# Linear attention on one core: every queue in a listed order, min and relu over two heads at once, copies and products in halves

## The chip, the core and the metric

The kernel runs on one core of a Trainium2 chip. The metric is the device time in microseconds (us) of one execution. The engines are PE (TensorE), ACT (ScalarE), DVE (VectorE), POOL (GpSimd) and SP, whose queue issues the DMA transfers. The program gives each engine a queue; each takes its instructions in the order written there and waits on semaphores for the others.

An execution is called slow when it is over 1.5% above the fastest of the same kernel; the slow ones of the changed kernel and its variants show a mean TensorE clock of about 0.96. Fast runs are compared with fast runs. The profile is a look at one of the executions; its "span" is about 1.8 us shorter than that execution's time.

## The reference

```python
B, H, S, D = 1, 32, 2048, 128            # q, k, v: bf16, normal * 0.05
def reference(q, k, v):
    phi_q = jnp.where(q > 0, q + 1, jnp.exp(q)) + 1e-6
    phi_k = jnp.where(k > 0, k + 1, jnp.exp(k)) + 1e-6
    kv  = jnp.einsum("bhsd,bhse->bhde", phi_k, v)
    z   = jnp.einsum("bhsd->bhd", phi_k)
    num = jnp.einsum("bhqd,bhde->bhqe", phi_q, kv)
    den = jnp.einsum("bhqd,bhd->bhq", phi_q, z)[..., None] + 1e-6
    return num / den
```

There are 32 heads, each with three loads of 512 KB and one store of 512 KB.

## The kernel before

phi is taken apart: phi(x) = min(exp(x), 1) + 1e-6 + max(x, 0). Both parts go through TensorE separately and add up in PSUM. Every head h needs the following work. The line numbers are those that the profiles show; they shift with the edits.

| work | engine | line before | line after |
|---|---|---|---|
| exp k (ek) | ACT | L190 | L320 |
| min of exp k, plus eps (em); relu k (rk) | DVE | L220; L222 | L304; L312 |
| copy v beside a column of ones (v1) | POOL | L236 | L349 |
| kv product, 32 matmuls (kv) | PE | L251 | L336 |
| copy of kv out of PSUM (kvs) | ACT | L215 | L342 |
| 16 transposes of q (T) | PE | L243 | L327 |
| exp q (eq); relu q, first half or all (rqa) | ACT | L194; L202 | L366; L369 |
| relu q, second half (rqb); min of exp q (emq) | DVE | L207; L227 | L372; L375 |
| numerator and denominator, 38 matmuls | PE | L259, L263, L265 | L268, L272, L274 |
| reciprocal (rA, rC), product over 12 or 4 tiles (fA, fC) | DVE | L293, L299 | L291, L295 |

In three heads of four, relu q is split between ACT and DVE; in every fourth, ACT takes all of it. The queues are filled by a loop, so an engine's order is the order of the calls in it:

```python
for i in range(NH):
    eq(i)                                # ACT
    ... rqa(i)                           # ACT (head 0 has extra work here; cut)
    if i + 1 < NH: kvs(i + 1)            # ACT
    if i + 2 < NH: ek(i + 2)             # ACT, two heads ahead
    if i >= 1:     f(i - 1, "A")         # DVE: rA, fA
    rqb(i); emq(i)                       # DVE
    if i >= 1:     f(i - 1, "C")         # DVE: rC, fC
    if i + 2 < NH: emrk(i + 2)           # DVE: min, relu of head i + 2
    if i + 1 < NH: T(i + 1)              # PE
    nA(i); nC(i)                         # PE: numerators, tiles 0-11 and 12-15
    if i + 2 < NH: kv(i + 2)             # PE
```

Two buffers hold each of exp k, relu k, v1, exp q, relu q and kvs. Eight slots hold loaded heads, six hold outputs. kv shares a PSUM bank with the numerators of tiles 14 and 15, so PE, ACT and DVE take turns on it. The v copy of head h waits for the kv product of h - 2 and for the numerator of h - 3:

```python
def v1(h):
    dep = [f"ldv{h}"]
    if h >= 2: dep += [f"kv{h - 2}"]
    if h >= 3: dep += [f"nA{h - 3}"]
    add("POOL", f"v1{h}", lambda e: e.tensor_scalar(v1_sb[:, h % 2, :, 0:D], v_sb[...], 1.0, 0.0,
        op0=ALU.mult, op1=ALU.add), dep)     # cut
```

Of the kernel before, what the change touches and what calls it, by code (L numbers as in the profile page):

```python
# [6 lines left out]
P = 128  # L7
# [8 lines left out]
class Program:  # L16
# [3 lines left out]
    def __init__(self, sem):  # L20
        self.sem = sem
        self.ops = {e: [] for e in ENGINES}
        self.where = {}
        self.count = {}
        self.sems = {}

    def add(self, eng, key, fn, deps=(), dma=None, inc=True):

        name = dma if dma is not None else eng
        if dma is not None or inc:  # L30
            self.count[name] = self.count.get(name, 0) + (16 if dma is not None else 1)
        if key is not None:
            assert key not in self.where, key
            assert dma is not None or inc
            self.where[key] = (name, self.count[name], eng, len(self.ops[eng]))
        self.ops[eng].append((fn, tuple(deps), name, (16 if dma is not None else 1) if (dma is not None or inc) else 0))

    def resolve(self):
        after = {}
        known = {e: {} for e in ENGINES}  # L40
        nxt = {e: 0 for e in ENGINES}
        cnt = {}
        self.plan = {e: [] for e in ENGINES}
        left = sum(len(o) for o in self.ops.values())
        while left:
            moved = False
            for e in ENGINES:
                while nxt[e] < len(self.ops[e]):
                    fn, deps, name, by = self.ops[e][nxt[e]]
                    need = [self.where[d] for d in deps]  # L50
                    if any((s, v) not in after for s, v, _, _ in need):
                        break
                    waits = {}
                    for s, v, _, _ in sorted(need, key=lambda t: -t[3]):
                        if known[e].get(s, 0) < v:
                            waits[s] = max(waits.get(s, 0), v)
                            for s2, v2 in after[(s, v)].items():
                                known[e][s2] = max(known[e].get(s2, 0), v2)
                    self.plan[e].append((fn, list(waits.items()), name, by))
                    if by:  # L60
                        cnt[name] = cnt.get(name, 0) + by
                        k = dict(known[e])
                        k[name] = max(k.get(name, 0), cnt[name])
                        after[(name, cnt[name])] = k
                    nxt[e] += 1
                    left -= 1
                    moved = True
            assert moved, {e: (nxt[e], self.ops[e][nxt[e]][1]) for e in ENGINES if nxt[e] < len(self.ops[e])}

    def emit(self, eng, engine):  # L70
        for fn, waits, name, by in self.plan[eng]:
            for s, v in waits:
                engine.wait_ge(self.get(s), v)
            ins = fn(engine)
            if by:
                ins.then_inc(self.get(name), by)

    def get(self, name):
        if name not in self.sems:
            self.sems[name] = self.sem()  # L80
        return self.sems[name]
# [16 lines left out]
def bass_standalone__linear_attn_elu__prompt_kernel(nc: bass.Bass, q: bass.AP, k: bass.AP, v: bass.AP, out: bass.AP):  # L98
# [8 lines left out]
    NO = 6  # L107
    LAG = 2

# [3 lines left out]
    with ExitStack() as es:  # L113
# [12 lines left out]
        em_sb, rk_sb = sb([P, 2, N]), sb([P, 2, N])  # L126
# [5 lines left out]
        ident, ones, epsr, one1 = sb([P, P]), sb([P, P]), sb([P, 3]), sb([P, 1])  # L132
# [4 lines left out]
        CO = 4 * 512  # L137

        def slot(t):
            if t < 12:  # L140
                return 512 * (t // 3) + NC * (t % 3)
            return CO + 512 * ((t - 12) // 2) + NC * ((t - 12) % 2)

        pr = Program(sem)
        add = pr.add
# [15 lines left out]
        def load(name, dst, src, h, freed):  # L161
            dep = [f"{f}{h - NI}" for f in freed] if h >= NI else []
            add("SP", f"ld{name}{h}", lambda e: e.dma_start(
                dst[:, h % NI].rearrange("p (j d) -> p j d", d=D), rows(src, h)), dep, dma=f"{name}{h % NI}")

        def loads(h):
            load("k", k_sb, kf, h, ["ek", "rk"])
            load("q", q_sb, qf, h, ["T"])
            load("v", v_sb, vf, h, ["v1"])

        def store(h):
            s = h % NO
            if h < NH - 1:
                add("SP", f"st{h}", lambda e: e.dma_start(rows(of, h), o_sb[:, s]), [f"fA{h}", f"fC{h}"], dma=f"o{s}")
            else:
                add("SP", None, lambda e: e.dma_start(rows(of, h)[:, 0:12, :], o_sb[:, s, 0:12]), [f"fA{h}"], dma=f"o{s}")
                add("SP", f"st{h}", lambda e: e.dma_start(rows(of, h)[:, 12:NT, :], o_sb[:, s, 12:NT]), [f"fC{h}"],
                    dma=f"o{s}")
# [3 lines left out]
        for h in range(NH + LAG):  # L182
            if h + NI < NH:
                loads(h + NI)
            if h >= LAG:
                store(h - LAG)


        def ek(h):
            add("ACT", f"ek{h}", lambda e: e.activation(em_sb[:, h % 2], k_sb[:, h % NI], ACT.Exp),  # L190
                [f"ldk{h}"] + ([f"kv{h - 2}"] if h >= 2 else []))

        def eq(h):
            add("ACT", f"eq{h}", lambda e: e.activation(emq_sb[:, h % 2], xT[:, :], ACT.Exp),  # L194
                [f"T{h}"] + ([f"nC{h - 2}"] if h >= 2 else []))
# [4 lines left out]
        def rqa(h):  # L200
            n = N // 2 if split(h) else N
            add("ACT", f"rqa{h}", lambda e: e.activation(rq_sb[:, h % 2, 0:n], xT[:, 0:n], ACT.Relu),  # L202
                [f"T{h}"] + ([f"nC{h - 2}"] if h >= 2 else []))

        def rqb(h):
            if split(h):
                add("DVE", f"rqb{h}", lambda e: e.tensor_scalar(  # L207
                    rq_sb[:, h % 2, N // 2:], xT[:, N // 2:], 0.0, None, op0=ALU.max),
                    [f"eq{h}"] + ([f"nC{h - 2}"] if h >= 2 else []))

        def rqs(h):
            return [f"rqa{h}"] + ([f"rqb{h}"] if split(h) else [])

        def kvs(h):
            add("ACT", f"kvs{h}", lambda e: e.activation(kvs_sb[:, h % 2], kv_ps, ACT.Copy),  # L215
                [f"kv{h}"] + ([f"nC{h - 2}"] if h >= 2 else []))

        def emrk(h):
            s = h % 2
            add("DVE", f"em{h}", lambda e: e.tensor_scalar(  # L220
                em_sb[:, s], em_sb[:, s], 1.0, EPS, op0=ALU.min, op1=ALU.add), [f"ek{h}"])
            add("DVE", f"rk{h}", lambda e: e.tensor_scalar(  # L222
                rk_sb[:, s], k_sb[:, h % NI], 0.0, None, op0=ALU.max), [f"ldk{h}"] + ([f"kv{h - 2}"] if h >= 2 else []))

        def emq(h):
            s = h % 2
            add("DVE", f"emq{h}", lambda e: e.tensor_scalar(  # L227
                emq_sb[:, s], emq_sb[:, s], 1.0, EPS, op0=ALU.min, op1=ALU.add), [f"eq{h}"])

        def v1(h):  # L230
            dep = [f"ldv{h}"]
            if h >= 2:
                dep += [f"kv{h - 2}"]
            if h >= 3:
                dep += [f"nA{h - 3}"]
            add("POOL", f"v1{h}", lambda e: e.tensor_scalar(  # L236
                v1_sb[:, h % 2, :, 0:D], v_sb[:, h % NI].rearrange("p (j d) -> p j d", d=D), 1.0, 0.0,
                op0=ALU.mult, op1=ALU.add), dep)

        def T(h):  # L240
            def f(e):
                for j in range(NT):
                    ins = e.transpose(xT[:, j * P:(j + 1) * P], q_sb[:, h % NI, j * D:(j + 1) * D], ident[:])  # L243
                return ins
            add("PE", f"T{h}", f, [f"ldq{h}", "ident"] + (([f"eq{h - 1}"] + rqs(h - 1)) if h else []))

        def kv(h):
            def f(e):
                for j in range(NT):
                    for part, src in ((0, em_sb), (1, rk_sb)):  # L250
                        ins = e.matmul(kv_ps, lhsT=src[:, h % 2, j * D:(j + 1) * D], rhs=v1_sb[:, h % 2, j, :],  # L251
                                       start=(j + part == 0), stop=(j == NT - 1 and part == 1))
                return ins
            add("PE", f"kv{h}", f, [f"em{h}", f"rk{h}", f"v1{h}", "v1ones0", "v1ones1"] + ([f"kvs{h - 1}"] if h else [])
                + ([f"fC{h - 3}"] if h >= 3 else []))

# [150 lines left out]
```

## Time and profile before

| | before |
|---|---|
| device time, median (range) of the first three runs | 201.49 us (199.21 to 203.07) |
| profiled span | 197.3 us |
| busy: PE, DVE, ACT | 86%, 82%, 81% |
| middle of the run, us per head | 5.52 |

From the page: the span, the engines' busy times with their share of the span, then two rows of 40 equal slices of the span, where each digit is tenths (9 is 90% or more).

```profile
span 197.3 us, 6384 instructions
PE 170.6 (86%) x2842; PEld 160.5 (81%) x2842; DVE 161.6 (82%) x254; ACT 160.0 (81%) x129; POOL 68.4 (35%) x38
PEclk9997999999999999999999999999999999999985
DMA  6999999999999999999999999999999622222133
```

No engine is full. The DMA row stands at 9 until about three quarters of the span and then falls to 2: the loads run ahead of the work and end at about 153 us. The TensorE clock dips at slice 3 (the fourth digit).

The timeline of ACT, from 71.8 us (start, duration, engine, line, operation, output<-input; in brackets the idle time before it and what ended it):

```profile
71.86 1.02 ACT L202 ACTIVATE la<-la 128x1024 bf16<-128x1024 bf16 x1
73.66 0.28 ACT L215 ACTIVATE la<-la 128x129 bf16<-128x129 f32 x1 [0.77 <-PE la L251]
73.83 1.90 ACT L190 ACTIVATE la<-la 128x2048 bf16<-128x2048 bf16 x1
75.64 1.87 ACT L194 ACTIVATE la<-la 128x2048 bf16<-128x2048 bf16 x1
77.39 1.88 ACT L202 ACTIVATE la<-la 128x2048 bf16<-128x2048 bf16 x1
79.19 0.28 ACT L215 ACTIVATE la<-la 128x129 bf16<-128x129 f32 x1
```

Read it from one kv copy (128x129) to the next: 73.66 to 79.19 is 5.53 us for one head. The first copy waited 0.77 us for the kv product. A head with half a relu on ACT (1.02 us) has about 4.65 us of ACT work, yet takes as long as a head with a whole one (1.88 us). So something other than ACT's own work sets the pace. The view of waits from 60 to 150 us (who waited for whom: us in total, times, longest):

```profile
ACT la L215 <- PE la L251: 9.2, 12, 0.8
DVE la L220 <- ACT la L190: 6.9, 16, 0.9
PE la L243 <- DVE la L207: 6.1, 12, 0.5
```

ACT waits for PE, DVE waits for ACT, PE waits for DVE: a ring. No one in it is slow; each stands idle in turn. The chain of waits goes round the same ring.

For later, the three DVE passes over 2048 bf16 columns in SBUF, from the groups by line and form (busy us, mean ns | idle before):

```profile
L220 DVE TENSOR_SCALAR la<-la 128x2048 bf16<-128x2048 bf16 x32 | 22.2, 694 | 27.4 <-ACT la L190 27.4
L222 DVE TENSOR_SCALAR la<-la 128x2048 bf16<-128x2048 bf16 x32 | 22.0, 687 | 0.0
L227 DVE TENSOR_SCALAR la<-la 128x2048 bf16<-128x2048 bf16 x32 | 21.8, 683 | 0.0
```

And, in the timelines of DVE and POOL, one relu k beside a v copy:

```profile
81.90 0.69 DVE L222 TENSOR_SCALAR la<-la 128x2048 bf16<-128x2048 bf16 x1
```

### The profile page before, as it was taken

Reading aid. Unit: us, or ns where it says so; the run is one execution under the profiler, and the core shown is the slowest. Engines: PE = TensorE matmul, PEld = TensorE weight load, DVE = VectorE, ACT = ScalarE, POOL = GpSimd, SP = SyncE. Lnnn points to the kernel's source line nnn. Section 1 sums busy time; section 2 is a strip of 40 time slices with the busy share of each in tenths; the row PEclk is TensorE's granted clock in tenths of the full one; section 3 lists DMA queues with packets and bytes.
Section 4 is the critical chain, followed back from the end, with each engine's and each line's share of the span. In section 5 each row is a group of like instructions: output and inputs, shape, how many; then the busy total and the mean of one; then the engine's idle time right before and its main releaser. Section 6 shows DMA issues by size and latency. Waiting matters only on the chain.

```text
span 197.3 us, 6384 instructions
## 1 busy us (share of the span) xinstructions
PE 170.6 (86%) x2842; PEld 160.5 (81%) x2842; DVE 161.6 (82%) x254; ACT 160.0 (81%) x129; POOL 68.4 (35%) x38
## 2 busy tenths in 40 slices
PE   6948999988898899988898889988898889988850
PEld 6938889888897889888897889888897889988850
DVE  0213899899989999899989999899989999899774
ACT  4563789988898889988898889988898889998530
POOL 1333343322344444332344444432344444431000
PEclk9997999999999999999999999999999999999985
DMA  6999999999999999999999999999999622222133
GB/s 228 346 418 411 412 404 407 410 404 416 416 411 422 412 416 419 411 420 414 414 420 413 419 418 414 419 414 417 416 415 394 246 116 110 106 106 105 61 130 137
DMA packets 18603, 67.52 MB, mean 342 GB/s; under 512 B 2064, under 2 KB 2192, under 8 KB 18576
## 3 DMA queue, kind: packets, MB, share of 16 engines
q1 hardware_dynamic: 18576, 67.12, 84.4%
q8 instruction: 22, 0.36, 0.7%
q14 instruction: 5, 0.04, 0.1%
HBM read 50.33 MB, written 16.78 MB: 340 GB/s over the span
## 4 chain that ended last, share of the span: by engine, by line
ACT 37%; PE 33%; DVE 22%; DMA 3%; issue 2%; POOL 1%; SPq 0%
ACT la L190 21%; PE la L251 18%; DVE la L299 9%; ACT la L202 6%; ACT la L194 6%; DVE la L220 6%; PE la L243 5%; PE la L263 5%; PE la L265 5%; DVE la L222 4%; DMA la<-in_v_dram 3%; ACT la L215 3%; DVE la L207 2%; DVE la L293 1%; POOL la L236 1%
## 5 line engine op out<-in xcount | busy, mean ns | idle before, releaser
L236 POOL TENSOR_SCALAR la<-la 128x2048 bf16<-128x2048 bf16 x32 | 67.7, 2116 | 109.1 <-PE la L265 97.5
L299 DVE TENSOR_TENSOR la<-la 128x1536 bf16<-128x1536 f32 x64 | 78.4, 1224 | 2.2
L251 PE MATMUL la<-la 128*128 128x129 bf16 x1024 | 65.3, 222 | 5.7 <-DVE la L222 5.4
L251 PEld LDWEIGHTS la<-la 128*128 128x128 bf16 x1024 | 59.7, 98 | 10.2 <-DVE la L222 7.1
L265 PE MATMUL la<-la 128*128 128x129 bf16 x512 | 66.7, 221 | 0.0
L263 PE MATMUL la<-la 128*128 128x129 bf16 x512 | 66.6, 220 | 0.0
L194 ACT ACTIVATE la<-la 128x2048 bf16<-128x2048 bf16 x32 | 59.8, 1869 | 3.7 <-PE la L243 3.7
L190 ACT ACTIVATE la<-la 128x2048 bf16<-128x2048 bf16 x32 | 60.9, 1902 | 1.9 <-DMA la<-in_k_dram 1.9
L265 PEld LDWEIGHTS la<-la 128*128 128x128 bf16 x512 | 49.8, 97 | 0.0
L263 PEld LDWEIGHTS la<-la 128*128 128x128 bf16 x512 | 47.6, 98 | 0.0
L243 PE MATMUL la<-la 128*128 128x128 bf16 x512 | 35.0, 222 | 12.7 <-DVE la L207 11.5
L220 DVE TENSOR_SCALAR la<-la 128x2048 bf16<-128x2048 bf16 x32 | 22.2, 694 | 27.4 <-ACT la L190 27.4
L243 PEld LDWEIGHTS la<-la 128*128 128x128 bf16 x512 | 29.6, 99 | 18.0 <-DVE la L207 15.5
L202 ACT ACTIVATE la<-la 128x1024 bf16<-128x1024 bf16 (+1 forms) x32 | 39.6, 1238 | 0.0
L259 PE MATMUL la<-la 128*128 128x3 bf16 (+1 forms) x192 | 32.5, 169 | 2.2 <-DVE la L227 2.2
L215 ACT ACTIVATE la<-la 128x129 bf16<-128x129 f32 x32 | 9.0, 280 | 23.0 <-PE la L251 23.0
L222 DVE TENSOR_SCALAR la<-la 128x2048 bf16<-128x2048 bf16 x32 | 22.0, 687 | 0.0
L227 DVE TENSOR_SCALAR la<-la 128x2048 bf16<-128x2048 bf16 x32 | 21.8, 683 | 0.0
L259 PEld LDWEIGHTS la<-la 128*128 128x128 bf16 x192 | 19.0, 99 | 2.4 <-DVE la L227 2.4
L207 DVE TENSOR_SCALAR la<-la 128x1024 bf16<-128x1024 bf16 x24 | 16.3, 681 | 0.0
L293 DVE RECIPROCAL la<-la 128x12 f32<-128x12 f32 x64 | 12.9, 201 | 2.5 <-PE la L265 2.5
L308 PE MATMUL la<-la 128*128 128x120 bf16 x90 | 7.6, 268 | 1.5 <-POOL la L149 1.5
(13 smaller groups left out, 9.9 us busy)
## 6 DMA issues: line engine op xcount, KB each, us to landing
la<-in_k_dram SPq DMA_DIRECT2D x32, 512.0 KB, 15.0
la<-in_q_dram SPq DMA_DIRECT2D x32, 512.0 KB, 15.0
la<-in_v_dram SPq DMA_DIRECT2D x32, 512.0 KB, 15.2
out_dram<-la SPq DMA_DIRECT2D x31, 512.0 KB, 15.1
out_dram<-la SPq DMA_DIRECT2D x1, 384.0 KB, 2.3
out_dram<-la SPq DMA_DIRECT2D x1, 128.0 KB, 2.1
```

Source lines behind the costliest of these rows:

```text
L190: add("ACT", f"ek{h}", lambda e: e.activation(em_sb[:, h % 2], k_sb[:, h % NI], ACT.Exp), [f"ldk{h}"] + ([f"kv{h - 2}"] if h >= 2 else []))
L194: add("ACT", f"eq{h}", lambda e: e.activation(emq_sb[:, h % 2], xT[:, :], ACT.Exp), [f"T{h}"] + ([f"nC{h - 2}"] if h >= 2 else []))
L202: add("ACT", f"rqa{h}", lambda e: e.activation(rq_sb[:, h % 2, 0:n], xT[:, 0:n], ACT.Relu), [f"T{h}"] + ([f"nC{h - 2}"] if h >= 2 else []))
L220: add("DVE", f"em{h}", lambda e: e.tensor_scalar(em_sb[:, s], em_sb[:, s], 1.0, EPS, op0=ALU.min, op1=ALU.add), [f"ek{h}"])
L222: add("DVE", f"rk{h}", lambda e: e.tensor_scalar(rk_sb[:, s], k_sb[:, h % NI], 0.0, None, op0=ALU.max), [f"ldk{h}"] + ([f"kv{h - 2}"] if h ...
L236: add("POOL", f"v1{h}", lambda e: e.tensor_scalar(v1_sb[:, h % 2, :, 0:D], v_sb[:, h % NI].rearrange("p (j d) -> p j d", d=D), 1.0, 0.0, o ...
L243: ins = e.transpose(xT[:, j * P:(j + 1) * P], q_sb[:, h % NI, j * D:(j + 1) * D], ident[:])
L251: ins = e.matmul(kv_ps, lhsT=src[:, h % 2, j * D:(j + 1) * D], rhs=v1_sb[:, h % 2, j, :], start=(j + part == 0), stop=(j == NT - 1 and par ...
L259: e.matmul(_ap(o_ps[:, :], slot(tiles[0]) + D, [[NC, n]]), lhsT=ones[:], rhs=epsr[:, 0:n], start=True, stop=False, skip_group_check=True)
L263: e.matmul(o, lhsT=emq_sb[:, s, t * P:(t + 1) * P], rhs=kvs_sb[:, s, :], start=False, stop=False, skip_group_check=True)
L265: ins = e.matmul(o, lhsT=rq_sb[:, s, t * P:(t + 1) * P], rhs=kvs_sb[:, s, :], start=False, stop=True, skip_group_check=True)
L299: add("DVE", f"f{which}{h}", lambda e: e.tensor_tensor(out=_ap(o_sb[:, :, :, :], ob + t0 * D, [[n * D, nb], [D, n], [1, D]]), in0=_ap(o_ps ...
```

## The change

The intent is to take each engine's order from a model that list-schedules the five queues, in place of one loop's order. What comes with it:

- Each queue, and the order of users of the shared PSUM bank, is a written list.
- exp k and relu k have four buffers each; min and relu of k run over two heads in one instruction from head 2 on.
- kv product, v copy and the numerator over 12 tiles come in two parts each.
- The v copies of heads 3 and 4 no longer wait for a numerator.
- The first load of k comes in halves; 35 warming matmuls replace 60 + 30; the last head runs in halves, with part of its division on ACT and three stores.

The core of the diff (heavily cut; the lists have 816 entries):

```diff
+    PAIRS_EM = 2
+    PAIRS_RK = 2
+    WARM = 35
+    SCHEDULE = dict(
+        PE=("warm0 T0 kx0 kv0 nA0 T1 kx1 kv1 nC0 T2 nB0 nC1 kx2 T3 kv2 nB1 nA1 nC2 kx3 kv3 nB2 nA2 T4 nC3 "
+            "kx4 kv4 nB3 nA3 T5 nC4 kx5 kv5 nB4 nA4 ..."),
+        DVE=("... rC4 rqb5 emq5 fC4 rA4 fA4 rqb6 rC5 emq6 fC5 rk9 rA5 fA5 emq7 rC6 fC6 em9 rA6 fA6 ..."),
+        ACT=("ek0.0 ek0 eq0 ek1 kvs0 rqa0 ek2 eq1 rqa1 kvs1 ek3 eq2 rqa2 ek4 kvs2 ek5 eq3 rqa3 kvs3 ek6 eq4 ..."),
+        POOL=("ident0 ident v10.0 v10.1 v11.0 v11.1 ..."),
+        kv=("... nC3 kx4 kv4 rC3 kvs4 fC3 nC4 ..."))      # order of users of the shared bank
-        em_sb, rk_sb = sb([P, 2, N]), sb([P, 2, N])
+        em_sb, rk_sb = sb([P, 4, N]), sb([P, 4, N])
+        def min_k(h, n):                                   # n = 2: two heads at once
+            add("DVE", key, lambda e: e.tensor_scalar(em_sb[:, s:s + n], em_sb[:, s:s + n], 1.0, EPS, ...
+        for r in range(2):                                 # v copy in halves
+            js = slice(8 * r, 8 * r + 8)
+            add("POOL", f"v1{h}.{r}", ...
+        num("B", h, (0, 1), ...)                           # numerator over 12 tiles in halves
+        num("A", h, (2, 3), ...)
```

Before, PE ran T(i+1), numerators of i, kv(i+2). Now it runs T(h+1), tiles 12 to 15 of h, kv(h+1), tiles 0 to 11 of h.

## The prediction

It was made from the profile of before and the diff, without a run of the changed kernel.

> **What bounds the kernel now.** No engine and not the DMA, but the order of the queues. The page gives PE 86%, DVE 82%, ACT 81% busy. In the timeline from 71 to 95 us, kv products start at 71.60, 77.12, 82.65 and 93.75 us: 5.53 us per head. Start-to-start times in the same timeline give each engine's own work per head:
>
> - ACT: exp k 1.80, exp q 1.76, relu q 0.92 (1.79 every fourth head), kv copy 0.18: about 4.9 us.
> - DVE: three 2048-wide passes at 0.61, relu half 0.61 on three heads of four, reciprocals 0.27 and 0.21, products 1.67 and 0.62: about 5.05 us.
> - PE: 32 kv matmuls, 16 transposes, 38 numerator matmuls at about 55 ns: 4.8 us.
>
> The chain of waits runs round a loop: kv copy, exp k, DVE min and relu (or exp q, relu q), kv product, kv copy. The waits view from 60 to 150 us shows its bubbles: ACT waits for the kv product 0.77 us in three heads of four, DVE for exp k 6.9 us over 16 heads, PE 0.5 us per split head for the DVE relu before the transposes.
>
> DMA is close behind. It is 99% busy at about 414 GB/s until the loads end near 153 us (slices of the page; the Trainium skill, "DMA: Bandwidth & Descriptors", Specifications, puts the fabric ceiling at 435 GB/s). At that rate 2.097 MB per head take an estimated 5.06 us. No DVE or ACT wait on a store or late load appears, since the loads are heads ahead.
>
> Outside the loop: the first numerator starts only at 19.6 us; after the last kv product (about 182 us) another 15 us pass.
>
> **What changes.** Work hardly changes. Pairing min and relu over two heads saves DVE an estimated 0.07 us twice per two heads, so DVE goes to about 4.97 us. Four em/rk buffers let exp k run ahead; the kv product moves to one head before its numerator, and the numerator of tiles 12 to 15 ahead of it, so that transposes, kv and numerators follow without the ACT/DVE round trip. Added: semaphore handoffs for the shared PSUM bank, one more POOL instruction per head.
>
> **Cost.** Steady state: I expect 5.08 us per head, DVE-bound with small handoff losses: 0.45 us less over about 29 heads, 13 us. Start: half-sized first k load, 35 instead of 90 warming matmuls and numerator 0 right after kv 0: an estimated 3 us earlier after losses. The end: last head in halves, its copies shared with ACT, three stores: about 3 us. Sum 19 us off 197.3 gives a span near 179, and with the 2 to 4 us between span and measured times **181.5 us**; eight in ten between **176 and 188**. Chances: faster 0.95, same 0.04, slower 0.01.
>
> **Right if** DVE's share is at or above 88% and ACT's near 87%; kv-product starts are about 5.1 us apart on average (uneven, as paired operations fall in every second head); ACT's wait for kv nearly vanishes; the first numerator starts by 14 us.
>
> **Wrong if**
> - DVE waits for stores: the six output slots free at the DMA's 5.06 us per head, and an estimate leaves 2 to 5 us of slack. Then DMA sets the pace, the period is 5.1 to 5.2, and the end is later.
> - The bank chain (kv, reciprocal, kv copy, product) makes ACT and DVE wait for each other each head: period 5.25 or more.
> - Fewer warming matmuls leave PE slow at the start: the Trainium skill, "TensorE: Matmul & The Clock Gate", Part 1, gives half clock until about 3.4 us of sustained work, and PE then idles for v until about 9 us. I allow 2 us; this trace's clock dips to 7 tenths at slice 3.
> - POOL half copies come late and hold kv.

## More of the kernel before

```profile
81.95 2.40 POOL L236 TENSOR_SCALAR la<-la 128x2048 bf16<-128x2048 bf16 x1 [3.13 <-PE la L265]
```

The relu starts 0.05 us ahead of the copy and takes its usual 0.69 us; the copy takes 2.40, where the mean is 2.12. This pair comes back in the experiments.

## The result

| | before | after |
|---|---|---|
| median (range) | 201.30 us (199.21 to 203.07), 4 runs | 180.79 us (179.58 to 182.96), 4 runs |
| profiled span | 197.3 us | 179.0 us |

The ratio of the fast runs is 0.8992, 95% interval 0.8888 to 0.9096. Ratios here are the mean time of one kernel's fast runs over that of the other's of the same rounds, so not quite the ratio of the medians. The kernel is 10% faster, and 180.79 lies in the predicted range (176 to 188, point 181.5).

The page of the changed kernel:

```profile
span 179.0 us, 6275 instructions
PE 162.2 (91%) x2787; PEld 155.8 (87%) x2787; DVE 157.2 (88%) x228; ACT 158.6 (89%) x134; POOL 80.3 (45%) x70
DMA  5999999999999999999999999999999999972325
```

DVE's and ACT's shares rose to 88% and 89%, and the DMA row holds 9 for 34 slices. The timeline of ACT, which answers to the one above:

```profile
96.02 0.29 ACT L342 ACTIVATE la<-la 128x129 bf16<-128x129 f32 x1
96.18 1.93 ACT L320 ACTIVATE la<-la 128x2048 bf16<-128x2048 bf16 x1
97.98 1.90 ACT L366 ACTIVATE la<-la 128x2048 bf16<-128x2048 bf16 x1
99.73 1.05 ACT L369 ACTIVATE la<-la 128x1024 bf16<-128x1024 bf16 x1
100.64 0.32 ACT L342 ACTIVATE la<-la 128x129 bf16<-128x129 f32 x1
```

From kv copy to kv copy it is now 4.62 us (96.02 to 100.64), and that is ACT's work for such a head. There is no gap between the lines. From the waits from 60 to 150 us (POOL's and those of weight loads left out):

```profile
PE la L268 <- DVE la L295: 1.4, 2, 1.1
DVE la L372 <- ACT la L366: 1.1, 4, 0.3
DVE la L295 <- ACT la L320: 1.0, 1, 1.0
ACT la L342 <- DVE la L291: 0.8, 1, 0.8
ACT la L342 <- DVE la L295: 0.8, 2, 0.5
DVE la L295 <- DMA out_dram<-la: 0.8, 2, 0.5
```

ACT's 9.2 us of waiting for kv products is gone. In these 90 us ACT waits 1.6 us for DVE, DVE 2.1 us for ACT and PE 1.7 us for DVE (0.3 us of it at the transposes, L327, not shown).

Where the 18.3 us of span came from can be read from the starts of the product over 12 tiles (1536 columns) of head 4 and of head 28, in the DVE timelines. Before:

```profile
44.09 1.76 DVE L299 TENSOR_TENSOR la<-la 128x1536 bf16<-128x1536 f32 x1
```

```profile
176.68 1.76 DVE L299 TENSOR_TENSOR la<-la 128x1536 bf16<-128x1536 f32 x1
```

After:

```profile
43.01 1.76 DVE L295 TENSOR_TENSOR la<-la 128x1536 bf16<-128x1536 f32 x1
```

```profile
163.19 1.76 DVE L295 TENSOR_TENSOR la<-la 128x1536 bf16<-128x1536 f32 x1
```

| stretch | before | after | difference |
|---|---|---|---|
| start to head 4 | 44.09 | 43.01 | -1.1 |
| head 4 to head 28 | 132.59 (5.52 per head) | 120.18 (5.01 per head) | -12.4 |
| head 28 to the end | 20.6 | 15.8 | -4.8 |

The middle gives two thirds.

### The profile page after: what moved, and what is told of

Same layout as the page of the kernel before. It is cut to its first block, busy times and chain, and to the rows that moved or that the text cites. A ratio compares the mean times of both kernels' runs of the same rounds, so it can differ in the third digit from the quotient of the medians.

```text
span 179.0 us, 6275 instructions
## 1 busy us (share of the span) xinstructions
PE 162.2 (91%) x2787; PEld 155.8 (87%) x2787; DVE 157.2 (88%) x228; ACT 158.6 (89%) x134; POOL 80.3 (45%) x70
## 4 chain that ended last, share of the span: by engine, by line
ACT 42%; DMA 27%; DVE 18%; SPq 4%; PE 3%; issue 3%; DVEq 0%
DMA out_dram<-la 17%; ACT la L320 16%; ACT la L366 16%; DMA la<-in_k_dram 10%; DVE la L295 9%; ACT la L369 8%; SPq L232 4%; DVE la L312 2%; DVE la L375 2%; DVE la L304 2%; ACT la L342 2%; DVE la L291 1%; DVE la L372 1%; PE la L336 1%; PE la L272 1%
## 5 line engine op out<-in xcount | busy, mean ns | idle before, releaser
L349 POOL TENSOR_SCALAR la<-la 128x1024 bf16<-128x1024 bf16 x64 | 79.6, 1261 | 83.8 <-PE la L274 69.6
L295 DVE TENSOR_TENSOR la<-la 128x512 bf16<-128x512 f32 (+2 forms) x64 | 77.7, 1213 | 3.9 <-DMA out_dram<-la 1.0
L274 PE MATMUL la<-la 128*128 128x129 bf16 x512 | 68.2, 220 | 0.0
L272 PE MATMUL la<-la 128*128 128x129 bf16 x512 | 68.1, 219 | 0.0
L336 PE MATMUL la<-la 128*128 128x129 bf16 x1024 | 65.3, 221 | 1.3 <-DVE la L291 0.6
L320 ACT ACTIVATE la<-la 128x2048 bf16<-128x2048 bf16 (+1 forms) x33 | 61.8, 1871 | 2.4 <-DMA la<-in_k_dram 2.4
L366 ACT ACTIVATE la<-la 128x2048 bf16<-128x2048 bf16 x31 | 58.6, 1891 | 5.3 <-PE la L327 5.2
L369 ACT ACTIVATE la<-la 128x1024 bf16<-128x1024 bf16 (+1 forms) x31 | 38.3, 1236 | 0.0
L327 PE MATMUL la<-la 128*128 128x128 bf16 x512 | 34.7, 222 | 2.7 <-DMA la<-in_q_dram 1.8
L327 PEld LDWEIGHTS la<-la 128*128 128x128 bf16 x512 | 30.4, 99 | 4.0 <-DMA la<-in_q_dram 2.0
L375 DVE TENSOR_SCALAR la<-la 128x2048 bf16<-128x2048 bf16 x31 | 21.0, 678 | 4.5 <-ACT la L366 4.5
L312 DVE TENSOR_SCALAR la<-la 128x4096 bf16<-128x4096 bf16 (+1 forms) x17 | 20.5, 1204 | 3.3 <-DMA la<-in_k_dram 3.1
L304 DVE TENSOR_SCALAR la<-la 128x4096 bf16<-128x4096 bf16 (+1 forms) x17 | 19.9, 1172 | 0.4 <-ACT la L320 0.4
L291 DVE RECIPROCAL la<-la 128x4 f32<-128x4 f32 (+2 forms) x65 | 12.9, 199 | 0.4 <-PE la L274 0.2
L408 PE MATMUL la<-la 128*128 128x120 bf16 x35 | 3.7, 307 | 1.5 <-POOL la L216 1.5
```

The lines of the kernel that those rows point to most:

```text
L272: e.matmul(o, lhsT=emq_sb[:, s, t * P:(t + 1) * P], rhs=kvs_sb[:, s, :], start=False, stop=False, skip_group_check=True)
L274: ins = e.matmul(o, lhsT=rq_sb[:, s, t * P:(t + 1) * P], rhs=kvs_sb[:, s, :], start=False, stop=True, skip_group_check=True)
L295: add("DVE", f"f{which}{h}", lambda e: e.tensor_tensor(out=_ap(o_sb[:, :, :, :], ob + t0 * D, [[n * D, nb], [D, n], [1, D]]), in0=_ap(o_ps ...
L312: add("DVE", key, lambda e: e.tensor_scalar(rk_sb[:, s:s + n], k_sb[:, b:b + n], 0.0, None, op0=ALU.max), [d for i in range(n) for d in ld ...
L320: add("ACT", "ek0.0" if h == 0 and r == 0 else f"ek{h}", lambda e, c=c: e.activation(em_sb[:, h % 4, c], k_sb[:, h % NI, c], ACT.Exp), ([f ...
L327: ins = e.transpose(xT[:, j * P:(j + 1) * P], q_sb[:, h % NI, j * D:(j + 1) * D], ident[:])
```

## The experiments

Twelve runs were made. Each was timed beside the kernel before, on three chips: runs 1, 2, 6 and 7 on one, 3, 4, 5 and 8 on another, 9 to 12 on a third (the kernel before has medians of 200.45, 201.37 and 200.68 us there). Against the kernel before, run 1 is slower, runs 2 and 6 are faster; run 7 has no verdict and the others are called unclear; on the last two chips ten of the eighteen runs of the kernel before were slow. The experiments are therefore compared with each other and with the changed kernel, by fast runs and profiles. Gaps between kv copies are read from the ACT timeline, as above.

### 1. The old order in the new program

The changed program, but its lists are built by the loop of before (min and relu cannot be paired in that order, which needs each head's kv product before the next head's exp k).

```diff
-    PAIRS_EM = 2
-    PAIRS_RK = 2
+    PAIRS_EM = NH
+    PAIRS_RK = NH
+    for i in range(NH):                  # cut: the order of before, for PE, DVE, ACT and the bank
+        act += [f"eq{i}", f"rqa{i}"] ...; act += [f"kvs{i + 1}"]; act += [f"ek{i + 2}"]
+        dve += [f"rA{i - 1}", f"fA{i - 1}", f"rqb{i}", f"emq{i}", f"rC{i - 1}", f"fC{i - 1}", f"em{i + 2}", f"rk{i + 2}"]
+        pe += [f"T{i + 1}", f"nB{i}", f"nA{i}", f"nC{i}", f"kx{i + 2}", f"kv{i + 2}"]
+    SCHEDULE.update(PE=pe, DVE=dve, ACT=act, kv=kvb)
```

> The changed program with everything it has (four em/rk buffers, half-sized first k load, 35 warming matmuls, halves, last head in halves) except two things: every engine's queue and the shared bank follow the order of the kernel before, and min and relu are not paired. Theory A (the order removed the round trip between ACT, DVE and PE): kv copies again about 5.5 us apart, ACT waiting for kv products again, span about 193 us: 4 us below before at most, from the start and the end. Rival B (start, end and buffers make the gain): period near 5.0 to 5.1 us, span below 184 us.

Measured: 209.85 us (209.34 to 211.12), ratio to before 1.048 (1.041 to 1.054), span 208.0 us. The ring is back, as theory A said: ACT waits for kv products again. But the kernel is 4.8% slower than before, not 4 us faster, so buffers, halves, start and end are worth less than nothing in the old order. The gaps are 5.60 us, and 6.48 us in every fourth head. The long gap, in the timelines of ACT, DVE and POOL:

```profile
89.78 0.28 ACT L381 ACTIVATE la<-la 128x129 bf16<-128x129 f32 x1 [1.73 <-PE la L375]
```

```profile
85.40 0.69 DVE L343 TENSOR_SCALAR la<-la 128x2048 bf16<-128x2048 bf16 x1 [0.88 <-ACT la L359]
86.01 1.57 DVE L351 TENSOR_SCALAR la<-la 128x2048 bf16<-128x2048 bf16 x1
```

```profile
85.99 2.50 POOL L388 TENSOR_SCALAR la<-la 128x1024 bf16<-128x1024 bf16 x2 [2.97 <-PE la L313]
```

The min takes 0.69 us as ever. The relu (L351 here, 2048 columns in SBUF) takes 1.57 us, and it starts at 86.01, just after two half copies of v start on POOL at 85.99. The Trainium skill has this: "SBUF — State Buffer", section "SBUF: two separate sides", says that a VectorE instruction that uses both of its ports and a GpSimd instruction lock each other out, and that whichever starts first keeps the ports for its whole instruction. The trace agrees, although no run shows directly which ports a pass uses: 1.57 us is the pass's own 0.69 and most of a half copy (a bit over 1 us). In the kernel before, the same relu started 0.05 us ahead of the copy (81.90 and 81.95) and was not held. Here it starts 0.02 us after it. A shift of 0.07 us between two starts costs the ring 0.9 us in every fourth head.

### 2. Pairing undone

```diff
-    PAIRS_EM = 2
-    PAIRS_RK = 2
+    PAIRS_EM = NH
+    PAIRS_RK = NH
+    # in DVE's list: "em3" becomes "em2 em3", and so on
```

> The changed kernel, min and relu once per head again, each pair split in place; order and all else kept. DVE does an estimated 0.075 us more per head. Theory A1 (DVE paces, as predicted): about 2 us longer, span 181 to 182. Rival A2 (ACT or DMA paces, DVE has about 0.05 us per head of slack): 0 to 1 us longer. Rival C (pairing, not order, makes the gain): 8 us or more longer.

Measured: 191.61 us (191.31 to 194.78, one slow run), ratio 0.955 (0.949 to 0.961), span 189.5 us, so 10.5 us above the changed kernel. A1 (2 us) and A2 (0 to 1) both missed; the size is that of rival C. Yet against the old order of run 1, also unpaired, the new order is worth 18 us. Both parts are needed. The timelines of DVE and POOL show where the pairs were lost:

```profile
98.20 2.13 DVE L307 TENSOR_SCALAR la<-la 128x2048 bf16<-128x2048 bf16 x2
```

```profile
98.57 2.66 POOL L352 TENSOR_SCALAR la<-la 128x1024 bf16<-128x1024 bf16 x2 [2.80 <-PE la L277]
```

Two mins take 2.13 us together; the changed kernel's paired min takes 1.22. The first starts before the copy. When it ends, the copy has begun, and the second stands still. In the changed kernel, one instruction over both heads starts just before the copy and holds the ports to its end:

```profile
91.27 1.22 DVE L304 TENSOR_SCALAR la<-la 128x4096 bf16<-128x4096 bf16 x1
```

```profile
91.28 3.12 POOL L349 TENSOR_SCALAR la<-la 128x1024 bf16<-128x1024 bf16 x2 [1.80 <-PE la L274]
```

Here POOL waits (3.12 us for the two halves, against 2.1 undisturbed), and POOL has time to spare.

### 3. The same without POOL's work

Run 2 with the v copy from head 4 on cut to one column per tile. The result is wrong; all waits stay.

```diff
-  v1_sb[:, s, js, 0:D], v_sb[...][:, js], 1.0, 0.0,
+  v1_sb[:, s, js, 0:W], v_sb[...][:, js, 0:W], 1.0, 0.0,      # W = D if h < 4 else 1
```

> The run called unpaired (191.6 us), with the v copy from head 4 on cut to one column per tile, so that POOL does almost nothing (result wrong on purpose; all waits stay). Theory P (unpaired lost its 10 us to VectorE passes that stand still while a POOL half copy runs: mean 872 and 853 ns against 694): the passes are back at 690 to 700 ns, span 180 to 183 us. Rival C2 (more instructions and waits of the unpaired queue made the loss): 187 us or more.

Measured: 183.43 us (181.94 to 184.60), span 182.7 us in a run at clock 0.961; the two runs at clock 1.0 took 181.94 and 182.31. Groups by line and form, run 2 first, then this one:

```profile
L315 DVE TENSOR_SCALAR la<-la 128x2048 bf16<-128x2048 bf16 x32 | 26.6, 872 | 2.9 <-DMA la<-in_k_dram 2.9
L307 DVE TENSOR_SCALAR la<-la 128x2048 bf16<-128x2048 bf16 x32 | 26.0, 853 | 0.4 <-ACT la L323 0.4
```

```profile
L315 DVE TENSOR_SCALAR la<-la 128x2048 bf16<-128x2048 bf16 x32 | 21.7, 716 | 2.9 <-DMA la<-in_k_dram 2.9
L307 DVE TENSOR_SCALAR la<-la 128x2048 bf16<-128x2048 bf16 x32 | 20.8, 688 | 0.4 <-ACT la L323 0.4
```

Theory P holds: the passes are back near 700 ns, and 8 to 9 us of the 10 us are gone (8 by the medians, 9 by the runs at a clock of 0.99 or more). The groups agree: (26.6 + 26.0) - (21.7 + 20.8) = 10.1 us less.

### 4. The changed kernel without POOL's work

The same edit on the changed kernel.

> The changed kernel with the same small v copy (result wrong on purpose). Theory P: pairing already left almost no collisions (4096-wide passes 1272 and 1211 ns against about 1220 undisturbed), so at most 2 us shorter than 179. Rival: POOL still holds VectorE back in every head; 4 us or more shorter.

Measured: 180.36 us (179.98 to 181.34), ratio 0.909, span 178.2 us. As theory P said, there was almost nothing left to gain. Run 3's two runs at full clock are about 2 us above this median: that is the work that pairing saves on DVE, and it is what the prediction put at 0.07 us per pass. The remaining 8 to 9 us of pairing's worth are collisions.

### 5. The old order without POOL's work

The same edit on run 1.

> The run called oldorder (209.9 us, kv copies 5.60 us apart and 6.48 in every fourth head) with the same small v copy (result wrong on purpose). If the order itself makes the bubbles and POOL only the 6.48: every gap 5.5 to 5.6, span 200 to 203 us, ACT still waiting 0.8 us for kv products. Rival (collisions make the old order slow altogether): period 5.2 or less, span below 192 us.

Measured: 204.66 us (204.25 to 205.12), ratio 1.031 (1.020 to 1.042), span 202.5 us. Gaps of 5.59 to 5.68 us in every head, and ACT waits 10.4 us for kv products from 60 to 150 us, 0.9 at most. This is as expected. Collisions made only the 6.48; the ring makes the rest. In the new program the ring is 0.08 us longer than the 5.52 of before. The timelines put 0.1 us of it between the transposes and the kv product (74.13 to 77.12 before, 95.84 to 98.92 in run 1).

### 6. The halves undone

One kv product, one v copy, one numerator over 12 tiles per head, except in the last head.

```diff
+    SCHEDULE["POOL"] = [k for k in SCHEDULE["POOL"] if not k.endswith(".0")]
+    for e in ("PE", "kv"):
+        SCHEDULE[e] = [k for k in SCHEDULE[e] if k[:2] != "kx" and not (k[:2] == "nB" and k != f"nB{L}")]
-            for r in range(2):
-                js = slice(8 * r, 8 * r + 8)
+            for r in range(1, 2):
+                js = slice(0, NT)
```

> The changed kernel with the halves undone in every head but the last: one kv product, one v copy, one product over 12 tiles per head. In the queue the halves stand side by side in every head but the first few and the last, so theory A expects no change: span within 1 us of 179. Rival: the early start of a half shortens the chain in each head; then 3 us or more longer.

Measured: 187.95 us (186.88 to 189.67), ratio 0.938, span 185.2 us: 6.2 us above the changed kernel. The size is that of the rival, but neither theory named the place. In the middle the gaps are the same (4.62 to 4.73 and 5.73). The loss is in the first heads: the third kv copy comes at 31.48 us, in the changed kernel at 25.31. From the timelines of ACT and PE:

```profile
31.48 0.28 ACT L345 ACTIVATE la<-la 128x129 bf16<-128x129 f32 x1 [4.46 <-PE la L340]
```

```profile
27.77 3.67 PE L340 MATMUL la<-la 128*128 128x129 bf16 x32
```

ACT waits 4.46 us for a kv product of 3.67 us, against 2.0 at full clock. A part of this is my edit's: in the list, the third head's halves stand on either side of T3, and I kept the later place. Which share belongs to the later first half of v, to that place and to the clock (0.953 to 0.982 in these four runs) was not separated.

### 7. Eight output slots

```diff
-    NO = 6
+    NO = 8
```

> The changed kernel with eight output slots instead of six. The chain of waits of the changed kernel puts 17% on stores, but DVE waits for stores 1.0 us in all. Theory A (engines pace; stores cost only those waits): 0.5 to 1.5 us shorter, the DVE wait for stores gone. Rival D (the DMA paces through the store slots): 3 us or more shorter, or the wait turns into a wait for loads.

Measured: fast runs 179.63 and 179.58 us, two slow ones 182.89 and 183.52; span 177.8 us, 1.2 us below the changed kernel's. The wait for stores is gone. The changed kernel first, then this one, at the product over four tiles of one head:

```profile
90.66 0.69 DVE L295 TENSOR_TENSOR la<-la 128x512 bf16<-128x512 f32 x1 [0.47 <-DMA out_dram<-la]
```

```profile
90.39 0.69 DVE L295 TENSOR_TENSOR la<-la 128x512 bf16<-128x512 f32 x1
```

As theory A said; D is out.

### 8. Fewer loads

q is loaded for eight heads only and used again (wrong; the comparison still passed, so the tolerance doesn't see q here).

```diff
-            load("q", q_sb, qf, h, ["T{}"])
+            if h < NI:
+                load("q", q_sb, qf, h, ["T{}"])
```

> The changed kernel without the loads of q from head 8 on (old q is used again; result wrong on purpose), so a quarter of the traffic in the middle is gone. Theory A (engines pace, DMA is only just enough): waits for stores gone, 0.5 to 2 us shorter, kv copies still about 4.93 us apart. Rival D (DMA at 99% paces): 4 us or more shorter.

Measured: fast runs 179.81, 180.92 and 179.81 us, ratio 0.9085; two slow runs; the profile is of a slow one (span 182.6). The gaps in the middle are 4.61 to 4.74 and 5.73, as with eight slots, 4.93 per head. From 100 to 140 us the DMA moves 303 GB/s instead of the 416 of the changed kernel, and the gaps stay. So traffic doesn't pace the changed kernel; A holds. The slow profile shows something else:

```profile
PEclk9955987999999999999999999999999999999999
```

The low clock lies in the first seven slices and nowhere else. The third kv copy comes at 30.71 us, not 25.31. Run 3's profile, also at 0.961, looks the same (third kv copy at 30.06). So what makes a run slow lies in its first heads; the slow runs of the changed kernel itself were not profiled.

### 9. and 10. Less work on ACT, less work on DVE

Both with eight slots, both wrong: exp k on three quarters of the columns; min of k on a quarter of them.

```diff
-  c = halves(r) if h == 0 else slice(0, N)
+  c = halves(r) if h == 0 else slice(0, N) if h < 4 else slice(0, 3 * N // 4)      # run 9
-  em_sb[:, s:s + n], em_sb[:, s:s + n], 1.0, EPS
+  em_sb[:, s:s + n, :NW], em_sb[:, s:s + n, :NW], 1.0, EPS                         # run 10; NW = N // 4 from head 4
```

> The changed kernel with eight output slots, exp k on three quarters of the columns from head 4 on (0.43 us less ACT work per head; result wrong on purpose). kv copies are 4.93 us apart with eight slots. If DVE alone paces: still 4.90 to 4.93. If ACT alone paces: 4.80, where PE's own work stands. If both are full, as their sums (4.86 and 4.97) say: 4.85 to 4.92, so less than 2 us off the span.

> The changed kernel with eight output slots, min over the paired heads on a quarter of the columns from head 4 on (an estimated 0.4 us less DVE work per head; result wrong on purpose). If DVE paces, as predicted: 4.87 us per head or less, ACT's own sum. If ACT paces: 4.90 to 4.93 as before, DVE waits for exp q grow instead.

Measured: run 9 180.36 us (178.72 to 182.37), run 10 181.33 us (180.88 to 185.10), with one slow run each. Four heads in the middle take 19.71 us with eight slots (kv copies at 71.40 and 91.11), 19.54 in run 9 (74.20 and 93.74), and 20.20 in run 10 (72.05 and 92.25). Busy time from 60 to 100 us (PE, PEld, DVE, ACT, POOL): run 9, then run 10.

```profile
60.00:100.00 40.00, 39.53 (x704) 38.38 (x702) 39.43 (x58) 37.69 (x34) 20.89 (x17) 1.00 1.03 415
```

```profile
60.00:100.00 40.00, 38.09 (x685) 37.36 (x683) 36.68 (x54) 38.80 (x33) 18.50 (x16) 1.00 1.03 415
```

Run 9 is as expected if both are full: 0.43 us less ACT work per head buys 0.04, because DVE is then busy 39.4 of 40 us. PE shows 39.5, but its matmuls overlap: from start to start, in run 7's timeline, they take an estimated 4.7 us of each head, which is less than the 4.89 of run 9. Run 10 fits neither expectation: less DVE work, a longer period. The fourth head of each four takes 6.22 us in it, not 5.73. DVE and POOL in that head, eight slots first:

```profile
86.44 1.22 DVE L312 TENSOR_SCALAR la<-la 128x4096 bf16<-128x4096 bf16 x1
```

```profile
86.51 3.06 POOL L349 TENSOR_SCALAR la<-la 128x1024 bf16<-128x1024 bf16 x2 [2.83 <-PE la L274]
```

```profile
87.10 1.70 DVE L313 TENSOR_SCALAR la<-la 128x4096 bf16<-128x4096 bf16 x1
```

```profile
86.67 3.03 POOL L350 TENSOR_SCALAR la<-la 128x1024 bf16<-128x1024 bf16 x2 [2.67 <-PE la L274]
```

With eight slots the relu wins by 0.07 us and takes 1.22. In run 10 it comes 0.43 us after the copy and takes 1.70. The time taken away upset the order of two starts, and the 0.48 us lost are what the fourth head grew by (0.49).

### 11. and 12. The changed kernel again, and one tuned by what was seen

Run 11 is the changed kernel. Run 12 has eight slots, 58 warming matmuls ahead of the first transposes, 25 ahead of the first kv product and 28 after it, and exp q of head 3 ahead of exp k of head 5.

```diff
-    NO = 6
+    NO = 8
-    WARM = 35
+    WARM = 58
+    a = SCHEDULE["ACT"]; i = a.index("ek5"); a[i:i + 2] = ["eq3", "ek5"]
+    a = SCHEDULE["PE"]; a.insert(a.index("T0") + 1, "warm1"); a.insert(a.index("kv0") + 1, "warm2")
```

> The changed kernel once more, for comparison on the same chip: 179.5 to 181 us in its fast runs; runs whose first products fall at half the TensorE clock (mean clock about 0.96) about 183 us.

> The changed kernel with eight output slots, exp q of head 3 ahead of exp k of head 5 (k 5 lands late), and 58 + 25 + 28 warming matmuls before the first transposes, before the first kv product and after it, in place of 35, to keep TensorE at full clock while it waits for loads. If slots and start are what is left: span 175 to 177 us, the third kv copy by 25 us in every run, no run at a mean clock below 0.98; about 2 us below the changed kernel's fast runs. If warming matmuls come to lie in the chain instead: 179 or more.

Measured: run 11 180.58 us (180.18 to 184.14, one slow run of six at clock 0.963), ratio 0.9036 (0.8977 to 0.9094). Run 12 181.55 us (181.27 to 181.69), ratio 0.9081 (0.9027 to 0.9136). The warming did what it was for, in that all six runs have a clock of 0.994 or more and lie within 0.4 us. But the time is no better than the fast runs of the changed kernel, and the third kv copy came at 25.72 us, later than I had said. The swap looks like a mistake. In the timeline of ACT:

```profile
27.48 1.88 ACT L373 ACTIVATE la<-la 128x2048 bf16<-128x2048 bf16 x1 [1.47 <-PE la L281]
```

exp q of head 3 waits 1.47 us for a numerator matmul (L281): it overwrites the buffer of head 1, whose numerators have just ended. In the changed kernel exp k of head 5 stands there. From the third kv copy to the fourth it is 7.09 us here, 6.56 in the changed kernel and 5.56 in run 7. So the written order seems right, and the one wait that I had looked at (exp k for its load, 0.86 us) hid a longer one. The three edits were not run apart. So no version shown here beats the changed kernel.

## Why the prediction was right

The time was right (181.5 against 180.79; span near 179 against 179.0), and so was the main mechanism, with its terms mis-sized. That the sum came within 1 us is partly luck: the start was put too high and the middle too low.

- **What bounds before: the order. Shown.** Putting the old order into the new program brought the ring back and 29 us with it of span (run 1 against the changed kernel), and with POOL quiet still 24 us (run 5 against run 4); pairing, undone with it, is about 2 us of these. The new buffers and halves alone do not do it, since run 1 has them too.
- **Steady state 5.08 us per head: too high.** Measured 5.01 over heads 4 to 28. The prediction's 0.45 us per head was 0.52.
- **DVE-bound: half right.** The sum of 4.97 us for DVE was near, but ACT is the fuller: with eight slots, from 60 to 140 us, it is busy 79.7 of 80 us and DVE 78.0. Three gaps of four are ACT's own 4.6 us, and the long one, 5.73, comes at the head whose whole relu q lies on ACT, not in every second head with the paired passes as forecast; with ACT relieved DVE takes over at once (run 9). Neither engine alone paces.
- **Pairing saves 0.07 us per pass: right as work, wrong as worth.** This is the step that the prediction missed. Runs 3 and 4 show about 2 us of saved work. Without pairing 10 us are lost, because passes and v copies collide (run 2). The prediction counted durations and didn't ask which passes would start while POOL holds the shared ports. Relative to before it gained no more than this work, since there the passes were undisturbed (683 to 694 ns on average); pairing keeps the new order from losing it.
- **Start, 3 us: measured 1.1.** The first numerator came at 13.88 us, as predicted, but only its second half; the product of head 0 started at 23.52 us, later than before (21.85). The stretch of 1.1 us also holds four heads at the shorter period, an estimated 2 us from 0.52 us each, so the start itself came later. Loads are one reason: the chain that ended last spends 17.3 us, up to 26.46, on a load of k. The shares of loads and of the clock were not separated.
- **End, 3 us: measured 4.8.** About 1.5 us of it are estimated to be three more heads at the shorter period. The last head's halves and the shorter distance between kv and numerator were sized together; they were not run apart.
- **Stores: the slack was real but thin.** DVE waited for stores three times, 1.0 us in the whole profile, and eight slots take that away (run 7). The DMA doesn't pace (run 8).
- **Warming: the warning was right.** Slow runs lose their time in the first heads (the profiles of runs 8 and 3), 2.2 to 4.6 us each against the fast runs of the same kernel. The Trainium skill, "TensorE: Matmul & The Clock Gate", Part 1, gives half clock until the array has been busy for a window; here the same 16 transposes took 1.89 us at the start of the changed kernel's profile and 1.06 later. The durations show it, not the profile's clock: that reads 1.00 from 6 to 10 us, where the 1.89 us lie.

Still open: what each of halves, place in the list and clock costs at the start (run 6); which of the moves in the lists opens the ring, since they were only undone together; and whether run 12 without its swap would win.

## What to carry to other kernels

When engines are each about 82% busy and wait for each other in a ring, look at the order of the queues before making any instruction faster. After reordering, check which VectorE passes now start beside a GpSimd instruction: a race of a few hundredths of a microsecond decides whether a pass takes 0.7 us or 1.6 us, and one wide instruction that starts first is safer than two. A queue that is full on two engines no longer answers to cuts on one, and a local swap that removes one visible wait can expose a longer one behind it.

## What the Trainium skill lacked or had wrong

- "GPSIMD Engine Reference", Key points, and "VectorE: DVE Perf Modes", Rules for kernel authors: neither says who waits in a collision; "SBUF — State Buffer" does. The runs show both directions: a pass of 0.69 us took 1.57 us when a half copy had started 0.02 us earlier, and two half copies took 3.12 us in place of 2.1 when a paired pass had started 0.01 us earlier.
- The pages cited here don't draw the rule from it that one wide pass is safer than two: two passes of 2048 columns took 2.13 us beside a copy, one of 4096 columns 1.22 us.
- "TensorE: Matmul & The Clock Gate", Part 1, puts the warm-up penalty below 1% of a typical span. Here the run at clock 0.963 took 184.14 us against 180.57 in the same rounds, 2.0%. That run was not profiled; in run 8's slow profile the low clock lies in the first heads only, and the third kv copy comes 5.4 us later than in the changed kernel's.
- "DMA: Bandwidth & Descriptors", Where 436 GB/s comes from: it says that for transfers between HBM and SBUF the HBM side, about 358 GB/s, binds. The table just above it and its note give up to 425 GB/s for a single core and about 358 for each of two that stream at once, so the sentence lacks this condition. In this program on one core, loads and stores together moved 416 GB/s from 60 to 140 us.
